# Moving q transposes, casts, a weight load and two batches' loads in a hand-ordered attention + FFN kernel

## The chip, the cores and the metric

The kernel runs on one core of one Trainium2 chip. The time is the device time of one launch in microseconds (us), the median of several runs. The engines are TensorE (PE: matmuls and transposes; its weight loads are listed apart as PEld), VectorE (DVE), ScalarE (ACT), GpSimd (POOL) and SyncE (SP). POOL and SP also issue DMAs, each into a queue of its own: the loads of this kernel go by POOL, the DMA transposes and the stores by SP. An engine works through its own instructions in order; a wait of one holds all that stand behind it on that engine.

## The reference, cut to what matters

```python
batch, n_heads, seq, head_dim = 8, 8, 576, 64
scores = q @ k.transpose(0, 1, 3, 2) / sqrt(D)
rel = pos[:, None] - pos[None, :]
mask_plain = (rel >= 0) & (rel < 32)                        # heads 0 to 3
mask_dil = (rel >= 0) & (rel < 128) & (rel % 4 == 0)        # heads 4 to 7
attn = softmax(where(mask, scores, -1e9))
x = (attn @ v).transpose(0, 2, 1, 3).reshape(4608, 512)     # 8 batches of 576 tokens
out = relu(x @ w_in) ** 2 @ w_out                           # w_in 512 x 2048, w_out 2048 x 512
```

Inputs are float32 in HBM; the matmuls run in bf16, and the loads cast on the way. The output is float32, 4608 x 512.

## The kernel before, in words

**Two halves laid into each other.** The FFN takes nearly all of PE's time; the attention of the eight batches supplies its input, xT (four slices kt of 128 rows, one for each pair of heads: 0 and 1 are the plain heads, 2 and 3 the dilated ones). The first 1024 tokens are four FFN tiles of 256 tokens, the rest tiles of 512. `ffn_groups` (L909) gives the groups of one tile: those of its first half, `g1` (L961), call `mm1` (L924), which multiplies w_in by xT over the four kt (the matmul is L937), then takes relu on ACT (L950) and the square on DVE (L953) into h2T; those of its second half, `g2`, multiply h2T by w_out (L983), copy PSUM to osb (L989) and store it on SP (L906). A tile of 256 tokens has 8 + 8 groups, one of 512 has 16 + 16. For the first two tiles the order is given by hand (`groups[:NF]` and the line behind it), and g1's first groups there take two u (two PSUM tiles pf) at once, and only two of the four kt: in the first tile groups 0 and 1 are the plain and the dilated kt of the first two u, and so on. So g1 can start when part of xT is there. The relus and squares of the first two u are not made at once but held, and let go by the code r (both relus, on ACT) and R (both squares, on DVE).

**Who sets the order.** At the end of the kernel a loop goes over the groups. After each it runs the codes of one cell of the string PROGRAM, and the steps of a list (`natural_step`, L674) that are due. PROGRAM's cells are split by "|"; the first runs before group 0, the next after group 0, and so on:

```python
    program = [x.split() for x in PROGRAM.split("|")]
    for code in program[0]:
        run(code)
    for g, group in enumerate(groups):
        ...
        group()
        for code in program[g + 1] if g + 1 < len(program) else ():
            run(code)
        while steps and steps[0][0] <= g:
            natural_step(*steps.pop(0)[2:])
```

What a code issues goes to the engines' instruction streams in that order; the codes that bear on the change are these.

- **Batch 0, part by part** (`first_step`): a code has a letter, a pair of heads 0 to 3, and a part of the tokens (0 is the first 256, 1 the rest). T transposes q and k on PE (L761, 16 transposes for q and 16 for k; "q" or "k" behind the code takes one alone); C copies the transposed halves from PSUM (DVE; an "a" behind it puts it on ACT, a "v" on DVE); S scores, E their Exp on ACT (L821) and the mask, P probabilities times v, D sums, L the Ln on ACT (L874), X the Exp of its negative (L877), M the product that writes xT on DVE (L884).
- **Casts**: h and j copy v's parts, loaded aside, into the block-diagonal vbd on DVE; j is two copies (L1096). G spreads a dilated v (L229).
- **Warm-up and filling** (`turn`, L731): s28x183 is 28 matmuls of 183 columns on an idle tile; w and W are single ones of 512 and 256 columns.
- **Loads**, codes that begin with L and a batch. q loads q and k of some pairs (L171, one DMA for q and one for k, 128 to 320 KB); v loads v, with "d" for the dilated heads and "p" for the plain ones (L192: four DMAs, two of each plain pair); V loads v of a later batch by `load_v_rows` ("d" is L465 and L470; "0" and "1" are the plain pairs 0 and 1, L478, eight DMAs for a pair). i and o load a quarter of w_in (L1055; "a" and "b" are the halves with kt 0, 1 and kt 2, 3) and of w_out (L1061). All of these are issued by POOL. x is the four DMA transposes of a batch's q and k, by SP (`cross`, L238), once its loads have landed. f loads the mask mask_n, by SP.

**The later batches.** Transposed q and k (qx, kx) are arranged by copies for the matmuls: L492 and L494 for the bulk, and the codes R for the ends of the rows, whose four pairs of DVE copies (L500 for q, L503 for k) write the tile that the trace calls kbd. `quadrants` issues the 64 x 64 matmuls of scores, sums and products (L661, into pa, pd and po); E is Exp (L698) and a mask product on DVE (L700, from batch 4 on by mask_n for the plain heads), and Ln, Exp, xT are L684 and the lines up to L689. Batch 3's copies R run near 83 us of the profiled execution, when POOL begins to issue batch 4's q and k loads; batch 4's R copies run before 111 us.

In this order POOL issues, around 70 to 90 us: L3:Vd0 (batch 3's dilated v and plain pair 0), L4:q00123 and L4:q10123 (batch 4's q and k, four DMAs), L3:V1 (batch 3's plain pair 1, eight DMAs). Ten groups later SP issues L4:x, and two cells on f.

Of the kernel before, what the change touches and what calls it, by code (L numbers as in the profile page):

```python
# [18 lines left out]


PROGRAM = (
    "L0:q001 L0:q023 L0:q123 L0:v0d L0:i0 L0:q101 L0:v1d L0:i1a L0:i1b L0:v1p L0:i2a L0:i2b L0:i3 L0:o0 L0:o1 L0:o2 L0:o3 "
    "L1:q00123 z y L1:v0dp L1:q10123 s28x183 T00 C00a T10 C10a B00 B10 w1 S00 E00 B20 W1 S10 E10 N u B30 W1 w1 T20q "
    "w1 T20k C20v T30 C30v h W1 w1 S20 E20 w1 S30 E30 T21 C21v T31 C31a G20 G30 P00 P10 D00 D10 L00 X00 P20 P30 "
    "D20 D30 L20 X20 M00 j S21 S31 w1+31 M20 E21 E31 G21 G31a | | T01 C01v r T11 C11a R P21 P31 D21 D31 S01 S11 L21 "
    "X21 M21 L31 X31 M31 E01 E11 | L2:q00123 L2:q10123 L1:v1dpr | | P01 D01 L01 X01 M01 P11 D11 L11 X11 M11 | | | "
    "| | | | | | | | | m n | | | | | | 1q1 1q3 | 1q2f 1k2f | 1k1a 1v3 | 1a2 | 1v2 1k0a 1q0v | 1o2 | 1a0 1a1 | 1k3 "
    "1o0 1o1f | 1a3 1Q0 | 1K0 1o3 | 1Q1 1K1 | 1Q2 | 1b0 | | 1Q3 1K2 L2:vwp L3:q00123 L3:q10123 L2:vwdr | L2:x | | "
    "| | 1V2 | 1b2 1p0 | 1b1 1V3 1K3 | L3:x | 1p2 1p1f | 1b3 | 2t0 2t1 1p3f | | | L3:Vd0 L4:q00123 L4:q10123 "
    "L3:V1 | | | | | | | | | | L4:x | | f | | | | | | | | | | | | | | | | L4:Vd L5:q10123 L5:q00123 L4:V01 | | | "  # L30
    "| | | | | | | | | | | | | L5:x | L5:Vd L6:q10123 L6:q00123 L5:V01"
)

# [29 lines left out]
def kernel(  # L63
# [21 lines left out]
    NE = H // 2  # L85
# [89 lines left out]
    def crossed(b: int, e: int):  # L175

        return int(b == XB and e in (1, 3) or b >= NATURAL and e == 1 or b >= PAIRED and e == 0)

    def load_v(b: int, parts, which="pdr"):


        dst = vbd[b % 2]
        if b not in vds:
            vds[b] = vd_pool.tile([P, NE // 2, 2, RES * D], bf16, name="vd")
        p0, p1 = parts[0], parts[-1] + 1
        i0, i1 = 4 * p0, 4 if p1 == 1 else NB
        sides = [(hl, slice(64 * hl, 64 * hl + 64)) for hl in range(2)]
        for what in which:
            if what == "p":
                for e in range(NE // 2):  # L190
                    for hl, rows in sides:
                        nc.gpsimd.dma_start(  # L192
                            dst[rows, e, i0:i1, rows],
                            v[b, 2 * e + (hl ^ crossed(b, e)), 64 * i0 : 64 * i1, :].rearrange("(i p) d -> p i d", p=64),
                        )
            elif what == "d" and len(parts) == 1:
                for hl, rows in sides:
                    nc.gpsimd.dma_start(
                        vds[b][rows, :, p0, :],
                        v[b, H // 2 + hl : H : 2, 256 * p0 : 256 * p1, :].rearrange("e (p r) d -> p e (r d)", r=RES),  # L200
                    )
            elif what in "d01":
                for e in (0, 1) if what == "d" else (int(what),):
                    for hl, rows in sides[::-1] if crossed(b, e + NE // 2) else sides:
                        hl = hl ^ crossed(b, e + NE // 2)
                        nc.gpsimd.dma_start(
                            vds[b][rows, e, :, :],
                            v[b, H // 2 + 2 * e + hl, 0:512, :].rearrange("(m p r) d -> p m (r d)", p=64, r=RES),
                        )
            elif b == XB:  # L210
                for g, rows in sides:
                    for i in (0, 8):
                        nc.gpsimd.dma_start(
                            dst[rows, NE // 2 : NE, i, rows],
                            v[b, H // 2 + g : H - g : 3 - 2 * g, 64 * i : 64 * i + 64, :].rearrange("h p d -> p h d"),
                        )
            elif p1 == 2:
                for hl, rows in sides:
                    nc.gpsimd.dma_start(
                        dst[rows, NE // 2 : NE, 8, rows],  # L220
                        v[b, H // 2 + hl : H : 2, 512:S, :].rearrange("h p d -> p h d"),
                    )
# [686 lines left out]
    def ffn_groups(tk0: int, nt: int):  # L909
# [6 lines left out]
        kts = (2, 0, 3, 1) if tk0 > 3 * NT else (2, 3, 1, 0) if tk0 == 2 * NT else (2, 3, 0, 1) if tk0 == 3 * NT else (0, 2, 1, 3) if NT <= tk0 < 2 * NT else (0, 1, 2, 3) if tk0 == 0 else (2, 3, 0, 1)  # L916
# [7 lines left out]
        def mm1(u, ks):  # L924
            if u not in acc:
                acc[u] = ps_f.tile([P, NT], f32, name="pf")
            for x in range(per):
                f = per * u + x
                piece = max(y for y in range(len(w_in_sb)) if w_cuts[y] <= P * f)
                c0 = 512 * (f // 4) + f % 4 - w_cuts[piece]  # L930
                for kt in ks:
                    t0 = tk0 % RING
                    to, rhs = acc[u][:, nt * x : nt * x + nt], xT[:, kt, t0 : min(t0 + nt, RING)]
                    if over:
                        to = to.rearrange("p (a t) -> p a t", a=2)
                        rhs = xT[:, kt, :].rearrange("p (a t) -> p a t", t=half)[:, 0 : t0 // half + 1 : t0 // half, :]
                    nc.tensor.matmul(  # L937
                        to,
                        w_in_sb[piece][:, kt, c0 : c0 + 509 : 4],
                        rhs,  # L940
                        start=(kt == kts[0] and x == 0),
                        stop=(kt == kts[-1] and x == per - 1),
                        skip_group_check=True,
                    )
            if ks[-1] != kts[-1]:
                return
            hv = h2[:, per * u : per * u + per, 0:nt]

            def relu():
                nc.scalar.activation(hv, acc[u][:, :].rearrange("p (x n) -> p x n", x=per), ACT.Relu)  # L950

            def square():
                nc.vector.tensor_tensor(out=hv, in0=hv, in1=hv, op=ALU.mult)  # L953

            if tk0 == 0 and u < 2:
                held.append((relu, square))
            else:
                relu()
                square()

        def g1(i):  # L961
            if i < 2 and tk0 < NT or i < 6 and tk0 == 0:
                x, y = divmod(i, 2)
                for u in (2 * x, 2 * x + 1):
                    mm1(u, kts[2 * y : 2 * y + 2])
            elif i < 2 and early:
                for u in (2 * i, 2 * i + 1):
                    mm1(u, kts[:cut])
            elif i < 4 and early:
                for u in (2 * i - 4, 2 * i - 3):  # L970
                    mm1(u, kts[cut:])
            else:
                mm1(i, kts)

        def g2(m, part):
# [11 lines left out]
            if f1 == NF:  # L987
# [3 lines left out]
                for x in (c0, DM // 2) if c1 - c0 == DM and tk0 == NTOK - NT else (c0,):  # L991
                    store(osb, pos, x, DM // 2 if x < c0 + DM // 2 and c1 - c0 == DM and tk0 == NTOK - NT else c1)

        return [lambda i=i: g1(i) for i in range(NF // per)] + [
            lambda m=m, part=part: g2(m, part) for m in range(nt // P) for part in range(4)
        ]
# [146 lines left out]
    for b in range(NATURAL, B):  # L1143
        t = G * (b - 1)
# [11 lines left out]
        if b < PAIRED:  # L1156
            start = 61 if early else t - 8
            second = t + (7 if early else 5)
            x = 3 if early else 0
# [89 lines left out]
```

## Time and profile before

| | us |
|---|---|
| runs | 298.61, 300.05, 300.09; median 300.05 |
| profiled execution, own time | 299.26 |
| profiled execution, span of the trace | 297.5 |
| PE busy in matmuls | 289.4 (97% of the span), 3150 instructions |
| of it L937 (w_in) and L983 (w_out) | 128.1 and 127.5 |
| ACT, DVE, POOL busy | 192.2 (65%), 168.5 (57%), 129.8 (44%) |
| L478, v loads, 80 issues on POOL | 43.4 |
| L171, q and k loads, 18 issues of q and 18 of k | 13.0 and 12.7 |
| granted clock of PE, mean | 0.997 of full speed |

The span runs from the first to the last recorded work; the execution's own time holds 1.76 us around it. All times of single instructions below are of this one profiled execution and count from the start of its span. "Busy" of an engine does not mean that it bounds: PE's waits, and what ended them, tell where work of others sets the time. The lines of a page's part 5 read: line of the kernel, engine, operation, what it writes <- what it reads, count, then busy time and mean of one in ns, then idle time of the engine just before, with what ended most of it. The rows of a wait list read: engine, tile and line that waited <- what it waited for (engine, tile, line), then the total in us, how often, and the longest. The rows of a timeline read: start in us, length in us, engine, line, operation, output <- input, shapes.

### The profile page before, as it was taken

Reading aid. Unit: us, or ns where it says so; the run is one execution under the profiler, and the core shown is the slowest. Engines: PE = TensorE matmul, PEld = TensorE weight load, DVE = VectorE, ACT = ScalarE, POOL = GpSimd, SP = SyncE. Lnnn points to the kernel's source line nnn. Section 1 sums busy time; section 2 is a strip of 40 time slices with the busy share of each in tenths; the row PEclk is TensorE's granted clock in tenths of the full one; section 3 lists DMA queues with packets and bytes.
Section 4 is the critical chain, followed back from the end, with each engine's and each line's share of the span. In section 5 each row is a group of like instructions: output and inputs, shape, how many; then the busy total and the mean of one; then the engine's idle time right before and its main releaser. Section 6 shows DMA issues by size and latency. Waiting matters only on the chain.

```text
span 297.5 us, 7863 instructions
## 1 busy us (share of the span) xinstructions
PE 289.4 (97%) x3150; PEld 169.2 (57%) x3177; DVE 168.5 (57%) x508; ACT 192.2 (65%) x397; POOL 129.8 (44%) x210
## 2 busy tenths in 40 slices
PE   8999999999999999999999999999999999999994
PEld 7689657869655554555455445545554555445443
DVE  2785566977879665686749474957445234004400
ACT  6898568767948665888667667766676567126511
POOL 8679883666786467564782697100000000000000
PEclk9999999999999999999999999999999999999998
DMA  8999999999999999969999499112101200121022
GB/s 126 196 168 213 205 156 228 187 175 167 186 132 171 178 166 168 196 95 147 156 192 151 61 177 167 10 37 73 37 0 35 75 35 0 37 71 35 0 74 71
DMA packets 83156, 35.37 MB, mean 119 GB/s; under 512 B 52656, under 2 KB 78512, under 8 KB 83120
## 3 DMA queue, kind: packets, MB, share of 16 engines
q0 software_dynamic: 49024, 18.40, 53.9%
q1 hardware_dynamic: 33952, 16.38, 26.3%
q8 instruction: 25, 0.41, 0.5%
q10 hardware_dynamic: 144, 0.10, 0.1%
q14 instruction: 11, 0.09, 0.1%
HBM read 37.31 MB, written 9.44 MB: 157 GB/s over the span
## 4 chain that ended last, share of the span: by engine, by line
PE 90%; DVE 3%; ACT 2%; DMA 2%; issue 1%; POOL 1%; ACTq 0%; POOLq 0%; DVEq 0%
PE pf L937 41%; PE pf L983 40%; DMA kb<-in_k_dram 2%; PE po L661 2%; PE pa L661 1%; PE pf L661 1%; PE pa L277 1%; PE pa L761 1%; DVE xT L884 1%; PE pd L661 1%; DVE kbd L503 0%; ACT rec L684 0%; POOL qb L171 0%; DVE h2T L953 0%; ACT h2T L950 0%
## 5 line engine op out<-in xcount | busy, mean ns | idle before, releaser
L937 PE MATMUL pf<-xT,w_in 128*128 128x512 bf16 (+1 forms) x697 | 128.1, 340 | 0.7 <-DVE xT L884 0.2
L983 PE MATMUL pf<-w_out_sb,h2T 128*128 128x512 bf16 (+2 forms) x572 | 127.5, 373 | 1.3 <-issue 0.5
L937 PEld LDWEIGHTS <-w_in 128*128 128x128 bf16 x704 | 77.9, 113 | 47.0 <-issue 1.1
L950 ACT ACTIVATE h2T<-pf 128x512 bf16<-128x512 f32 x144 | 83.7, 600 | 29.5 <-PE pf L937 29.3
L953 DVE TENSOR_TENSOR h2T<-h2T 128x512 bf16<-128x512 bf16 x144 | 60.3, 425 | 60.1 <-ACT h2T L950 57.7
L983 PEld LDWEIGHTS <-h2T 128*128 128x128 bf16 x592 | 55.6, 98 | 61.5
L478 POOL DMA_DIRECT2D vbd<-in_v_dram x80 | 43.4, 556 | 23.4 <-DMA kb<-in_k_dram 9.0
L989 ACT COPY osb<-pf 128x512 f32<-128x512 f32 (+1 forms) x34 | 19.5, 573 | 49.7 <-PE pf L983 46.6
L171 POOL DMA_DIRECT2D qb<-in_q_dram x18 | 13.0, 721 | 11.4 <-DMA xx<-qb 9.4
L684 ACT ACTIVATE rec<-rec 128x576 f32<-128x576 f32 x24 | 16.4, 682 | 0.7
L698 ACT ACTIVATE pt<-pa 128x384 bf16<-128x384 f32 (+1 forms) x28 | 12.7, 498 | 6.2 <-DVE xT L689 3.7
L192 POOL DMA_DIRECT2D vbd<-in_v_dram x16 | 10.9, 690 | 7.6 <-DMA kb<-in_k_dram 2.9
L465 POOL DMA_DIRECT2D vd<-in_v_dram x20 | 12.2, 621 | 4.0 <-DMA vbd<-in_v_dram 2.7
L687 DVE TENSOR_TENSOR xT<-po,rec 128x512 bf16<-128x512 f32 x14 | 9.7, 691 | 7.5 <-ACT rec L684 7.1
L171 POOL DMA_DIRECT2D kb<-in_k_dram x18 | 12.7, 705 | 1.9 <-issue 0.7
L700 DVE TENSOR_TENSOR pt<-pt,mask_n 128x448 bf16<-128x448 bf16 (+1 forms) x20 | 7.1, 373 | 9.5 <-ACT pt L698 9.4
L470 POOL DMA_DIRECT2D vbd<-in_v_dram x20 | 12.2, 628 | 0.1
L700 DVE TENSOR_TENSOR pt<-pt,mask_f 128x384 bf16<-128x384 bf16 x24 | 8.4, 355 | 6.0 <-ACT pt L698 5.8
L687 DVE TENSOR_TENSOR xT<-pf,rec 128x512 bf16<-128x512 f32 x10 | 6.9, 692 | 8.4 <-ACT rec L684 8.4
L492 DVE COPY qT<-xx 64x576 bf16<-64x576 bf16 (+1 forms) x30 | 10.7, 357 | 0.6
L661 PEld LDWEIGHTS <-vbd 64*64 64x64 bf16 x288 | 7.6, 107 | 4.2 <-issue 3.8
L698 ACT ACTIVATE pt<-pf 128x448 bf16<-128x448 f32 (+1 forms) x18 | 8.5, 521 | 0.5 <-PE pf L661 0.3
(156 smaller groups left out, 317.7 us busy)
## 6 DMA issues: line engine op xcount, KB each, us to landing
qb<-in_q_dram POOLq DMA_DIRECT2D x7, 320.0 KB, 7.2
kb<-in_k_dram POOLq DMA_DIRECT2D x7, 320.0 KB, 7.9
vd<-in_v_dram POOLq DMA_DIRECT2D x32, 64.0 KB, 4.8
w_out_sb<-in_moe_w_out_dram POOLq DMA_DIRECT2D x4, 512.0 KB, 11.5
out_dram<-osb SPq DMA_DIRECT2D x16, 128.0 KB, 4.9
qb<-in_q_dram POOLq DMA_DIRECT2D x7, 256.0 KB, 6.8
kb<-in_k_dram POOLq DMA_DIRECT2D x7, 256.0 KB, 8.5
out_dram<-osb SPq DMA_DIRECT2D x9, 160.0 KB, 3.1
```

The lines of the kernel that those rows point to most:

```text
L171: nc.gpsimd.dma_start(t[0:n, part, hs, :], src[b, hs, t0 : t0 + RES * n, :].rearrange("h (p r) d -> p h (r d)", r=RES))
L478: nc.gpsimd.dma_start(v_rows[b % 2][p0 + 16 * r : p0 + 16 * r + 16, e, :, :], v[b, 2 * e + hl, :, :].rearrange("(i m r) d -> r m i d", r=R ...
L661: nc.tensor.matmul(out, lhs, rhs, start=begin, stop=True, skip_group_check=True)
L684: nc.scalar.activation(rec[:, :], rec[:, :], ACT.Exp, scale=-1.0)
L687: nc.vector.tensor_tensor(out=tok[:, :, 16:M], in0=byr(o[:, :]), in1=byr(rec[:, 0:512]), op=ALU.mult)
L698: nc.scalar.activation(pt, sp[b, e][g][:, 0:n], ACT.Exp, scale=SCALE)
L700: nc.vector.tensor_tensor(out=pt, in0=pt, in1=mask, op=ALU.mult)
L937: nc.tensor.matmul(to, w_in_sb[piece][:, kt, c0 : c0 + 509 : 4], rhs, start=(kt == kts[0] and x == 0), stop=(kt == kts[-1] and x == per - ...
L950: nc.scalar.activation(hv, acc[u][:, :].rearrange("p (x n) -> p x n", x=per), ACT.Relu)
L953: nc.vector.tensor_tensor(out=hv, in0=hv, in1=hv, op=ALU.mult)
L983: nc.tensor.matmul(cur[m][:, c0:c1], h2[:, f, P * m : P * m + P], w_out_sb[:, f, c0:c1], start=(f == 0), stop=(f == NF - 1),)
L989: (nc.vector.tensor_copy if last and part == 1 or tk0 == 3 * NT // 2 else nc.scalar.copy)(osb[:, c0:c1], cur[m][:, c0:c1])
```

## The change

1. The warm-up is 34 matmuls of 151 columns instead of 28 of 183.
2. The load of batch 0's later plain v (L0:v1p, four DMAs) is split into its pairs, "s" and "t" (two DMAs each), which `load_v` now takes. The first half of w_in's third quarter (L0:i2a) is issued between them: v pair 0, i2a, v pair 1, i2b instead of v pairs 0 and 1, i2a, i2b.
3. The two casts j go from behind M00 (xT of pair 0, part 0) to between C21v and T31, that is on DVE ahead of the copy C31 and of all products of part 0.
4. The q transposes of the plain pairs' second part, T01q and T11q, go from behind group 1 to between group 0 and group 1; the k transposes T01k and T11k stay behind group 1. The two held relus r go from between C01v and T11 to behind C11a, and so behind it on ACT.
5. In the second tile (tokens 256 to 511, kt order 2, 3, 0, 1) the group g1(1), which adds kt 0 and kt 1 to the first two u, goes kt by kt: the four matmuls of kt 0 for both u, then the four of kt 1, instead of u by u with kt 0 and kt 1 in turn. In the trace of before its first two matmuls start at 24.53 and 24.88.
6. L3:V1, eight DMA issues, goes ahead of L4:q00123 and L4:q10123 on POOL.

Nothing is added to or taken from what is computed.

```diff
-    "L0:q001 L0:q023 L0:q123 L0:v0d L0:i0 L0:q101 L0:v1d L0:i1a L0:i1b L0:v1p L0:i2a L0:i2b L0:i3 L0:o0 L0:o1 L0:o2 L0:o3 "
-    "L1:q00123 z y L1:v0dp L1:q10123 s28x183 T00 C00a T10 C10a B00 B10 w1 S00 E00 B20 W1 S10 E10 N u B30 W1 w1 T20q "
-    "w1 T20k C20v T30 C30v h W1 w1 S20 E20 w1 S30 E30 T21 C21v T31 C31a G20 G30 P00 P10 D00 D10 L00 X00 P20 P30 "
-    "D20 D30 L20 X20 M00 j S21 S31 w1+31 M20 E21 E31 G21 G31a | | T01 C01v r T11 C11a R P21 P31 D21 D31 S01 S11 L21 "
+    "L0:q001 L0:q023 L0:q123 L0:v0d L0:i0 L0:q101 L0:v1d L0:i1a L0:i1b L0:v1s L0:i2a L0:v1t L0:i2b L0:i3 L0:o0 L0:o1 L0:o2 L0:o3 "
+    "L1:q00123 z y L1:v0dp L1:q10123 s34x151 T00 C00a T10 C10a B00 B10 w1 S00 E00 B20 W1 S10 E10 N u B30 W1 w1 T20q "
+    "w1 T20k C20v T30 C30v h W1 w1 S20 E20 w1 S30 E30 T21 C21v j T31 C31a G20 G30 P00 P10 D00 D10 L00 X00 P20 P30 "
+    "D20 D30 L20 X20 M00 S21 S31 w1+31 M20 E21 E31 G21 G31a | T01q T11q | T01k C01v T11k C11a r R P21 P31 D21 D31 S01 S11 L21 "
...
-    "| | 1V2 | 1b2 1p0 | 1b1 1V3 1K3 | L3:x | 1p2 1p1f | 1b3 | 2t0 2t1 1p3f | | | L3:Vd0 L4:q00123 L4:q10123 "
-    "L3:V1 | | | | | | | | | | L4:x | | f | | | | | | | | | | | | | | | | L4:Vd L5:q10123 L5:q00123 L4:V01 | | | "
+    "| | 1V2 | 1b2 1p0 | 1b1 1V3 1K3 | L3:x | 1p2 1p1f | 1b3 | 2t0 2t1 1p3f | | | L3:Vd0 L3:V1 L4:q00123 L4:q10123 "
+    "| | | | | | | | | | L4:x | | f | | | | | | | | | | | | | | | | L4:Vd L5:q10123 L5:q00123 L4:V01 | | | "
...
-            if what == "p":
-                for e in range(NE // 2):
+            if what in "pst":
+                for e in {"p": (0, 1), "s": (0,), "t": (1,)}[what]:
...
         def g1(i):
             if i < 2 and tk0 < NT or i < 6 and tk0 == 0:
                 x, y = divmod(i, 2)
-                for u in (2 * x, 2 * x + 1):
-                    mm1(u, kts[2 * y : 2 * y + 2])
+                for ks in [kts[2:3], kts[3:]] if tk0 and y else [kts[2 * y : 2 * y + 2]]:
+                    for u in (2 * x, 2 * x + 1):
+                        mm1(u, ks)
```

## The prediction

> **What bounds the kernel now.** First the page's part 1 and part 4, for who is busy and who stands on the chain of work that ended last; then PE's waits; then timelines of the two stretches where PE waits.
>
> ```profile
> PE 289.4 (97%) x3150; PEld 169.2 (57%) x3177; DVE 168.5 (57%) x508; ACT 192.2 (65%) x397; POOL 129.8 (44%) x210
> ...
> PE 90%; DVE 3%; ACT 2%; DMA 2%; issue 1%; POOL 1%; ACTq 0%; POOLq 0%; DVEq 0%
> ```
>
> PE is the bound: no edit takes PE work away, so only its 8 us of waits can be won. They are, from PE's waits:
>
> ```profile
> PE po L731 <- DVE kbd L1005: 1.1, 1, 1.1
> PE pa L661 <- DVE kbd L503: 0.5, 1, 0.5
> PE pf L983 <- issue: 0.5, 3, 0.2
> PE pf L813 <- issue: 0.4, 1, 0.4
> PE pf L937 <- DVE xT L884: 0.2, 1, 0.2
> PE pa L761 <- DMA kb<-in_k_dram: 0.2, 1, 0.2
> ```
>
> The first is the start, before any edit. Two of the others lie where edits bear: L937 on xT (15.90 us) and, the largest, L661 on the kbd copies of L503 (84.75 us). From DVE's timeline, columns start, length, what (pairs of L500 and L503 copy the ends of batch 3's q and k), and POOL's:
>
> ```profile
> 77.90 0.19 DVE L500 COPY kbd<-xx 64x128 bf16<-64x128 bf16 x1
> 78.01 0.30 DVE L503 COPY kbd<-xx 64x128 bf16<-64x128 bf16 x1
> ...
> 83.39 0.58 DVE L503 COPY kbd<-xx 64x128 bf16<-64x128 bf16 x1
> 83.98 0.19 DVE L500 COPY kbd<-xx 64x128 bf16<-64x128 bf16 x1
> 84.09 0.60 DVE L503 COPY kbd<-xx 64x128 bf16<-64x128 bf16 x1
> ```
> ```profile
> 82.46 0.70 POOL L171 DMA_DIRECT2D qb<-in_q_dram  x1
> 83.14 0.69 POOL L171 DMA_DIRECT2D kb<-in_k_dram  x1
> 83.81 0.76 POOL L171 DMA_DIRECT2D qb<-in_q_dram  x1
> 84.54 0.75 POOL L171 DMA_DIRECT2D kb<-in_k_dram  x1
> 85.25 2.70 POOL L478 DMA_DIRECT2D vbd<-in_v_dram  x5
> ```
>
> The same copy takes 0.30 us in general (L503: 294/303/604 ns least, median, most) and 0.58 and 0.60 only here, beside POOL's issues of L171, batch 4's q and k loads. PE waits for the second of these to end. That is the stall that the moved loads touch.
>
> **The change part by part.**
>
> *Warm-up, 34 matmuls of 151 columns for 28 of 183.* The 28 take 4.47 us, 153 ns apart, 0.84 ns a column. 34 x 151 = 5134 columns against 5124: 0.01 us. Twelve more PE instructions stand ahead of everything, so the 0.44 "issue" wait at 13.97, which no semaphore explains, may move. It is worth nothing either way: the first FFN group starts at 14.63 behind xT (L884, 13.89 + 0.69 = 14.58), whose DVE and ACT chain does not need that matmul. Value 0; ends 0 and, if it came to lie where nothing covers it, 0.44 lost.
>
> *The two casts (j, L1096) ahead of batch 0's last k cast, and the q transposes between groups 0 and 1.* Now xT of heads 0 to 3 ends at 14.58, j takes 0.29 and 0.22, and the xT of the dilated heads runs 15.15 to 15.84; PE has stood 0.24. Moved to 12.05, the casts fall into 0.39 us of idle DVE ahead of L770 and 0.15 us more; L229's first copy, 0.45 against 0.22 for the next, ends with POOL's L192 as it does now, so xT moves by 0 to 0.1. The second xT is then ready by 15.6, and PE, with 16 transposes (0.31) in between, comes at about 16.1: no wait, 0.24 won. The price is one more turn between L937 and the 64-row L761: the rows leave 0.09 ahead of the transposes and 0.10 behind them, 0.19 in all. Sum 0.05 won.
>
> *Relus (r) behind C11a on ACT.* Now the two relus (1.08) run at 16.82, C11a at 17.79, and L874 at 18.54 after 0.31 idle. As built, C11a comes first and waits for the transposes of k, which end at about 17.6; C11a 0.43, two relus 1.08: L874 at about 19.1, 0.5 late. Queued behind it on ACT are Ln, Exp and the scores' Exp; xT of head pair 3 (20.34 to 20.83) ends at about 21.3, and group 4's second matmul reads it at 21.08. PE would wait 0.2 to 0.4. PSUM of the two relus comes free at 19.1, just as the next pair needs it (19.2). Value 0.3 lost; ends 0 and 0.45.
>
> *Pair by pair order in the four groups of g1(1) at token 256.* Now the second matmul there starts 0.35 behind the first (24.53, 24.88), where 0.11 is the pace: 0.24 of wait for xT of pair 1 (L884, 24.33 + 0.49 = 24.82). Four matmuls of pair 0 first give 0.44 of cover. 0.24 won, as long as the Ln/Exp chain is late only by what PE is.
>
> *Half of w_in[2] ahead of v's second pair.* The bytes ahead of the second half stay, so it lands as before (needed at 23.65); the first half lands 0.5 sooner, needed 22.8; the v pair 1.3 later, at about 22.2, needed at 22.3. PE never waited for w_in here. Value 0; ends 0 and 0.2 lost.
>
> Front: 0.05 - 0.3 + 0.24, so **about 0**, ends -0.6 and +0.3. A loss is not eaten later: from 25.6 to 84 PE hardly waits.
>
> *Batch 4's q and k loads behind batch 3's v (L3:V1).* Eight issues of L478, 0.53 each, come at 82.46 and L171 only at 86.7. Beside the copies POOL then runs L478. Bounds for a copy beside L478, by its rows: 0.30 (106.51, 109.92), 0.33 (77.08), 0.40 (110.34). Two copies at 0.30 to 0.40 for 0.58 and 0.60: 0.4 to 0.6 less. PE's wait in pace is 0.69 (84.06 to 84.75), so all of it counts. Value **0.5 won**.
>
> *What that makes late.* The loads issue 4.3 later, but land less than that later: the rings run at 30 to 52 GB/s from 82 to 85 us and two stores (SP, 83.4) are out of the way. kb's first part now takes 5.9 us (issue 83.14; POOL's wait for it ends at 89.3); the fastest 128 KB loads of the start took 4.4. It lands 2.8 to 4.3 later; I take 3. SP's transposes wait for it (89.08, four, SP's last ends at 97.92), the mask_n load (97.97, 4.3 to landing, 102.3) is queued behind them, stores behind that. With 3 more, less some competition, it lands at 104.9 (104.2 to 106.6). Who waits: DVE's L700 on pt and mask_n, now at 104.43, and behind it the copies of batch 4's ends, xT, and three more pairs, the last ending at 110.74; PE reads that at 110.92. DVE idles 1.45 in between (108.26, for ACT), so the mask may land at 105.8 for nothing, at 105.4 with PE 0.5 sooner. Value 0; ends 0 and 1.2 lost. Batch 5's loads start about 3 later, its transposes (now 115.42, behind stores) under 1; its copies at 131 have 3 us of slack. v's second pair comes sooner and is needed only at 110.
>
> [...]
>
> **Sum.** 0 + 0.5 - 0 (0.1 at a mean over the mask's ends): 0.45 won. Against the profiled execution (297.5 span, 299.26 with what lies around it): 298.8. That execution lies 0.79 under the median of the three runs (300.05) and between them (298.61 to 300.09); the middle of all four is 299.65, so I forecast **299.2** for a median.
>
> **The rivals** (times on the same footing as 299.2).
> *A. L478 holds the copies as long as L171.* For: 0.43 and 0.40 us in two rows of a copy that meets the end of an issue, and back-to-back issues always offer one. Against: most rows at 0.30. Only the front is left: 299.65.
> *B. The mask comes late; slower.* It decides from 105.9: there the stall of L661 at 110.9 equals what was won at 84.75. For: the transposes of batch 3 took 67.8 to 76.7 on SP and more to land, some 2 us longer than batch 4's, in rings as full. With loads 3.6 later and such transposes the mask lands at 108.0, L700 to the last pair takes 2.0 + 0.43 + 1.10 + 1.37, PE reads at 113.0 for 110.92: 2.1 lost, 301.7. Against: rings are emptier then.
> *C. The relus cost nothing*, because C11a gets its transposes sooner or the late xT is hidden: front +0.3, in all 0.8 won, 298.9.
> That the change does not do what it says: the built order shows each move; of the casts alone PE's 0.24 would be gone.
>
> **How the numbers follow.** Forecast 0.5, A 0.15, B 0.15, C 0.2. 8 in 10: C's 298.9 with the runs' spread (0.75 either way) below, half of B left out above: 298.1 to 300.9. Half a per cent, 1.5 us, is about what a measurement of this kernel can tell from no change. No case wins 1.5; a median's spread on C gives faster 0.1. B is 1.65 over 300.05: slower 0.1. Within: 0.8.
>
> **What would show it.** L503 at 83.4 and 84.1 at 0.30 to 0.40, L661's wait on it under 0.2; L937's wait at 15.90 gone, the pause at 24.88 gone; L874 at 19.1 and a wait of L937 at 21; L171 at 86.7, mask_n landing near 104.9, no wait of L661 near 110.5. It is wrong if L503 stays at 0.58 (A), if L661 waits at 110 to 113 (B), or if PE's total wait falls by over 1 us.

## The result, and the profile after

The changed kernel takes 301.17 us (median of 19 runs, 299.70 to 304.32), the kernel before beside it 299.40 (19 runs, 298.48 to 301.79): ratio 1.0061, 95% interval 1.0039 to 1.0084. It is 0.6% slower, where 299.2 was forecast, and the time lies outside the range (298.1 to 300.9). Slow runs, over 1.5% above the fastest of their kernel, are left out of the ratios here and below: one of these 19 (304.32), and three of the six with the mask loaded three times. The execution that was profiled is the fastest of the 19: its own time is 299.70, its span 297.9.

First the page of the changed kernel, parts 1 and 4. From L966 on a line's number is higher by one than before (L983 is now L984).

```profile
PE 290.1 (97%) x3156; PEld 169.6 (57%) x3183; DVE 167.7 (56%) x508; ACT 192.0 (64%) x397; POOL 129.3 (43%) x210
...
PE 75%; DMA 13%; POOL 5%; DVE 2%; issue 2%; ACT 1%; SPq 0%; ACTq 0%; DVEq 0%; POOLq 0%
```

No engine's busy time moved by more than 0.8 us, but the chain that ended last did: before, PE held 90% of it and DMA 2%, now PE holds 75% and DMA and POOL 18%. So the chain leaves PE somewhere. Its pieces in order of time (start, length, what) show where it comes back:

```profile
88.20 7.50 DMA qb<-in_q_dram
...
95.98 5.91 DMA vbd<-in_v_dram
101.89 0.38 SPq L238
102.33 4.01 DMA mask_n<-near_by_residue
106.43 0.67 DVE pt L700 x2
...
108.76 0.69 DVE xT L687
...
110.88 0.42 DVE kbd L503
111.34 0.22 PE pa L661 x3
111.72 5.99 PE pf L984 x27
```

PE is late at 111.34 because the last copy L503 ends at 111.30, and that stands on DVE behind L700, which waited for mask_n. The mask is issued at 102.33 and lands at 106.34; L700 begins 0.09 later, as it does in the three other traces in which the mask is late. (The timeline of this one execution names ACT's L680 for that wait, which happened to end at 106.35; the first experiment tells the two apart.) In the profile of before the mask landed at 102.29, and L700 waited for ACT's Exp (L698) until 104.43. SP's queue in the two kernels, before first, says why the mask is late (start, length, line):

```profile
89.08 1.24 SPq L238 DMA_TRANSPOSE xx<-kb  x1
90.41 3.07 SPq L238 DMA_TRANSPOSE xx<-qb  x1
93.59 2.63 SPq L238 DMA_TRANSPOSE xx<-kb  x1
96.31 1.61 SPq L238 DMA_TRANSPOSE xx<-qb  x1
97.97 1.15 SPq L1100 DMA_DIRECT2D mask_n<-near_by_residue  x1
```
```profile
92.35 1.84 SPq L238 DMA_TRANSPOSE xx<-kb  x1
94.28 3.69 SPq L238 DMA_TRANSPOSE xx<-qb  x1
98.07 2.74 SPq L238 DMA_TRANSPOSE xx<-kb  x1
100.90 1.37 SPq L238 DMA_TRANSPOSE xx<-qb  x1
102.33 1.27 SPq L1101 DMA_DIRECT2D mask_n<-near_by_residue  x1
```

What SP waited for before the first of them, in the changed kernel (from 86 to 108 us):

```profile
SPq L238 <- DMA kb<-in_k_dram: 7.9, 1, 7.9
```

The four transposes begin 3.27 later, behind kb's later landing (92.30 for 89.03), take 9.92 instead of 8.84 from the first start to the last end, and the mask is queued behind them. The chain above goes back from the last transpose to a load of vbd; SP's queue does not bear that out, since each transpose there starts within 0.1 of the end of the one before.

What was to be won at 84.75 was won. DVE's copies of the same ends in the changed kernel, now beside POOL's L478, not L171:

```profile
83.19 0.18 DVE L500 COPY kbd<-xx 64x128 bf16<-64x128 bf16 x1
83.29 0.30 DVE L503 COPY kbd<-xx 64x128 bf16<-64x128 bf16 x1
83.60 0.19 DVE L500 COPY kbd<-xx 64x128 bf16<-64x128 bf16 x1
83.71 0.30 DVE L503 COPY kbd<-xx 64x128 bf16<-64x128 bf16 x1
```

And PE's waits no longer name L503 at 85:

```profile
PE po L731 <- DVE kbd L1006: 1.1, 1, 1.1
PE pf L937 <- DVE xT L884: 0.6, 1, 0.6
PE pf L984 <- issue: 0.5, 3, 0.2
PE pa L761 <- DMA kb<-in_k_dram: 0.3, 1, 0.3
```

The 0.6 on xT is the first FFN matmul, at 14.70: the wait of 0.44 at 13.97 that the profile of before calls "issue" is gone, and PE waits for the same xT as before. The list does not name the loss at 111, because it is spread over a row of matmuls. Between the FFN matmuls on its two sides, the block of L661 takes from 110.06 to 111.29 before, 1.23, and now from 109.50 to 111.72, 2.22. Its matmuls wait one after the other for DVE, none of them for long.

The sum, from the start of the same FFN matmuls in both traces: the first FFN matmul 0.07 later, 0.18 won from there to 25 us, 0.58 won at 85, 1.11 lost at 111: 0.42 later to the end, which is the 0.4 between the spans. That is the fastest of 19 executions; the median lies 1.5 above it.

### The profile page after: what moved, and what is told of

Read it like the earlier page. It is cut to its first block, busy times and chain, and to the rows that moved or that the text cites. A ratio compares the mean times of both kernels' runs of the same rounds, so it can differ in the third digit from the quotient of the medians.

```text
span 297.9 us, 7875 instructions
## 1 busy us (share of the span) xinstructions
PE 290.1 (97%) x3156; PEld 169.6 (57%) x3183; DVE 167.7 (56%) x508; ACT 192.0 (64%) x397; POOL 129.3 (43%) x210
## 4 chain that ended last, share of the span: by engine, by line
PE 75%; DMA 13%; POOL 5%; DVE 2%; issue 2%; ACT 1%; SPq 0%; ACTq 0%; DVEq 0%; POOLq 0%
PE pf L937 34%; PE pf L984 34%; DMA kb<-in_k_dram 5%; DMA vbd<-in_v_dram 5%; DMA qb<-in_q_dram 3%; POOL vbd L478 2%; DMA mask_n<-near_by_residue 1%; PE po L661 1%; POOL qb L171 1%; PE pf L661 1%; PE pa L661 1%; PE pa L761 1%; PE pa L277 1%; ACT h2T L950 1%; POOL vbd L192 0%
## 5 line engine op out<-in xcount | busy, mean ns | idle before, releaser
L984 PE MATMUL pf<-w_out_sb,h2T 128*128 128x512 bf16 (+2 forms) x572 | 127.5, 373 | 1.3 <-issue 0.5
L984 PEld LDWEIGHTS <-h2T 128*128 128x128 bf16 x592 | 55.6, 98 | 61.5
L478 POOL DMA_DIRECT2D vbd<-in_v_dram x80 | 42.9, 546 | 20.2 <-DMA qb<-in_q_dram 8.0
L171 POOL DMA_DIRECT2D qb<-in_q_dram x18 | 12.9, 718 | 12.8 <-DMA xx<-qb 11.3
L698 ACT ACTIVATE pt<-pa 128x384 bf16<-128x384 f32 (+1 forms) x28 | 12.8, 499 | 6.1 <-DVE xT L689 3.6
L470 POOL DMA_DIRECT2D vbd<-in_v_dram x20 | 12.0, 614 | 6.0 <-DMA qb<-in_q_dram 2.6
L700 DVE TENSOR_TENSOR pt<-pt,mask_n 128x448 bf16<-128x448 bf16 (+1 forms) x20 | 7.0, 372 | 12.1 <-ACT pt L698 7.4
L171 POOL DMA_DIRECT2D kb<-in_k_dram x18 | 12.9, 716 | 1.8 <-issue 0.8
L687 DVE TENSOR_TENSOR xT<-po,rec 128x512 bf16<-128x512 f32 x14 | 9.7, 691 | 5.6 <-ACT rec L684 5.3
L465 POOL DMA_DIRECT2D vd<-in_v_dram x20 | 12.1, 617 | 1.4 <-DMA vbd<-in_v_dram 1.3
L700 DVE TENSOR_TENSOR pt<-pt,mask_f 128x384 bf16<-128x384 bf16 x24 | 8.4, 355 | 6.3 <-ACT pt L698 6.2
L687 DVE TENSOR_TENSOR xT<-pf,rec 128x512 bf16<-128x512 f32 x10 | 6.9, 691 | 8.8 <-ACT rec L684 8.8
L661 PEld LDWEIGHTS <-vbd 64*64 64x64 bf16 x288 | 7.9, 107 | 4.6 <-issue 3.5
L661 PE MATMUL po<-pt,vbd 64*64 64x96 bf16 (+2 forms) x188 | 8.8, 201 | 0.1
```

Of the source, the lines that this page charges most:

```text
L171: nc.gpsimd.dma_start(t[0:n, part, hs, :], src[b, hs, t0 : t0 + RES * n, :].rearrange("h (p r) d -> p h (r d)", r=RES))
L478: nc.gpsimd.dma_start(v_rows[b % 2][p0 + 16 * r : p0 + 16 * r + 16, e, :, :], v[b, 2 * e + hl, :, :].rearrange("(i m r) d -> r m i d", r=R ...
L661: nc.tensor.matmul(out, lhs, rhs, start=begin, stop=True, skip_group_check=True)
L687: nc.vector.tensor_tensor(out=tok[:, :, 16:M], in0=byr(o[:, :]), in1=byr(rec[:, 0:512]), op=ALU.mult)
L698: nc.scalar.activation(pt, sp[b, e][g][:, 0:n], ACT.Exp, scale=SCALE)
L700: nc.vector.tensor_tensor(out=pt, in0=pt, in1=mask, op=ALU.mult)
```

## The experiments

Theory M: the loss is the mask alone. It is late because its load is queued on SP behind transposes that wait for later loads; each us beyond 105.4 is lost at 111. Theory T: batch 4's later transposes themselves hold DVE, and the mask only stands beside them. Theory F: the front costs in most executions what the profiled one does not show.

**The mask load ahead of the transposes, in the changed kernel.**

```diff
-... | L4:x | | f | ...
+... | f L4:x | | | ...
```

> The changed kernel, with the load of mask_n issued by SP ahead of batch 4's four transposes and not behind them; nothing else. Theory M (the mask is late because it is queued on SP behind transposes that wait for later loads, and every us that it lands after about 105.4 is lost at the wait of L661 near 111): what was won at 84.75 (0.58) and in front (0.1) stays, and nothing is lost: 0.5 to 0.8 faster than before, L700 on mask_n about 104, no wait of L661 near 111, and a spread of runs as narrow as that of before. Theory T (batch 4's transposes themselves land too late for the copies R on DVE, and the mask only stands beside them): DVE then waits at 106 to 108 for L500 instead, and 0 to 1.5 slower than before. Theory F (the front costs in most runs what the profiled run does not show): about 1 slower than before whatever the mask does.

Measured: 298.78 (12 runs, 298.43 to 301.11), before beside it 299.56; ratio 0.9990 (0.9973 to 1.0008), so the 0.6% is gone; a gain over before is not shown, since the interval includes no change. Its DVE timeline:

```profile
103.73 0.74 DVE L700 TENSOR_TENSOR pt<-pt,mask_n 128x448 bf16<-128x448 bf16 x2 [1.94 <-ACT pt L698]
```

L700 waits for ACT again. The transposes are as late as in the changed kernel (SP's last ends at 102.33, it lands at 105.11) and PE has no wait at 111: T falls, M stands.

**The moved loads of batches 3 and 4 alone, in the kernel before.**

```diff
-... L3:Vd0 L4:q00123 L4:q10123 L3:V1 ...
+... L3:Vd0 L3:V1 L4:q00123 L4:q10123 ...
```

> The kernel before with one edit alone: L3:V1 ahead of batch 4's q and k loads. Theory M and theory T: as slow as the whole change, 1.3 to 2.2 slower than before, with the wide spread of runs, mask_n landing at 106 or later. Theory F: 0.5 faster than before or within 0.3 of it.

Measured: 302.77 (6 runs, 300.60 to 303.62); ratio 1.0108 (1.0076 to 1.0140). The mask lands at 108.58. So this part alone makes the loss; that it is larger than that of the whole change (301.17) was not expected. Its trace shows a second price, in a table of stretches (window; length, then PE, PEld, DVE, ACT, POOL busy, granted clock, DMA share, GB/s):

```profile
109.60:111.80 2.20, 0.03 (x1) 0.06 (x1) 2.13 (x9) 0.00 (x0) 1.45 (x3) 1.00 0.61 99
111.80:114.20 2.40, 2.20 (x90) 1.52 (x90) 1.63 (x8) 0.70 (x2) 2.40 (x5) 0.99 1.23 218
114.20:117.60 3.40, 3.40 (x10) 1.21 (x9) 2.13 (x6) 1.98 (x5) 1.00 (x3) 0.51 1.44 195
117.60:120.00 2.40, 2.40 (x13) 1.10 (x12) 1.14 (x4) 0.59 (x1) 0.75 (x2) 1.00 1.40 139
```

PE stands for 2.2 us, and 2.4 us after it resumes the granted clock is 0.51 for 3.4 us: eight matmuls start 0.43 apart instead of 0.22, another 1.7 lost. That the wait brought this on is my reading of this one trace.

**Everything but the moved loads.** The changed kernel with L3:V1 back behind batch 4's loads.

> The changed kernel with L3:V1 put back behind batch 4's q and k loads, so that all other parts are in. Theories M and T: within 0.3 of before, narrow spread (the profiles of the two kernels differ by 0.1 up to 84 us). Theory F: 1 or more slower than before.

Measured: 298.83 (12 runs, 298.17 to 299.50); ratio 0.9974 (0.9957 to 0.9991): faster, where M had "within 0.3" and F "1 slower". F falls. The mask lands at 103.11, in time. This is the one of twelve comparisons that is faster clear of its interval.

**The changed kernel once more.**

> The changed kernel once more, for the profile of another execution and beside the other three on one chip. All theories: 1.2 to 2.4 slower than before. Theory M: where its time is above that of the first profile (299.70), the mask_n load lands later than 106.34 by as much, and the wait of L661 near 111 is longer by as much. Theory F: the more lies ahead of 84 us.

Measured: 300.41 (12 runs, 298.93 to 302.22); ratio 1.0029 (1.0000 to 1.0058). That is 0.9 above before's 299.56 in this set, less than any theory had, and about half the loss of the first measurement (1.0061); between the two sets the size of the loss is not settled better than 0.3 to 0.6%. The profiled execution, 301.39, has the mask at 107.76, 1.42 later than the first profile, and PE's wait list names L661:

```profile
PE po L661 <- DVE xT L687: 1.1, 1, 1.1
```

At 111 it lost 2.1, against 1.1: 1.0 more for 1.42 of the mask, with PE 0.6 later there, so that the mask was due later too. Most of the rest of its 1.69 lies at the start (first FFN matmul at 15.25 for 14.70), which is F's place and not M's.

**The mask load first, in the kernel before.** The edit of the first experiment, in the kernel before.

> The kernel before with one edit: the load of mask_n ahead of batch 4's transposes on SP. Theory M (only the mask's lateness costs; where the kernel before runs over 301 it was late there too): the median within 0.4 below that of before, no run over 300.5. Theory S (the kernel before has its own slow executions for another reason, as in its front): the same median and as many runs over 300.5 as before has (8 of 29). Rival to M on this point: a transfer of 114 KB at 84 us in the way of batch 4's loads makes it slower by up to 0.5.

Measured: 299.25 (12 runs, 298.61 to 300.63), before 299.30; ratio 0.9997 (0.9978 to 1.0016). Two of the 12 runs lie over 300.5, where M had none; of before, two of 29 do in this set, and five of 29 in the set that the expectation counts (not eight). So it is S on this point: in the old order the mask is rarely the limit, and three of 12 runs over 300 with the mask first show that such runs have other causes too. The rival's 0.5 is not there.

**The relus back ahead of C11a**, in the changed kernel with the mask first.

```diff
-T01k C01v T11k C11a r R
+T01k C01v r T11k C11a R
```

> The changed kernel with the mask load first and the two relus r put back ahead of C11a on ACT. Term of the relus as predicted (0.3 lost; 0.21 in the traces so far, between the groups at 19.2 and 21.1): the time from the first FFN matmul to 25 us is 0.2 to 0.3 shorter than with the relus behind C11a, and the whole 0.2 to 0.3 faster than the kernel with the mask load first (298.78), so 298.5. If the late xT is hidden anyway: no difference.

Measured: 299.13 (12 runs, 298.33 to 300.56); ratio to before 0.9991 (0.9973 to 1.0010), for the whole time no difference that can be told. The trace tells it: from the first FFN matmul to the 111th (near 30.6 us) it takes 15.67, and 15.85 or 15.86 in all six traces with the relus behind C11a, and PE's wait near 21 is gone. The term is 0.18.

**The mask load twice, and three times, in the kernel before.**

```diff
-... | L4:x | | f | ...
+... | L4:x | | f f | ...
+... | L4:x | | f f f | ...
```

> The kernel before, with the load of mask_n issued twice in a row on SP (the second waits for the first to land, and L700 for the second); load order and all else as before. It delays the mask alone, with batch 4's loads and transposes where they were. Theory M: the last landing is near 105.5 to 106.5; the wait at 110.9 is 0 to 0.6 and the time 0 to 0.6 above that of before, with more runs above 301. Theory T (it is batch 4's loads and transposes that count): no difference from before.

Measured: 299.79 (12 runs, 298.62 to 303.00); ratio 1.0018 (0.9994 to 1.0043). The mask lands at 105.91, and nothing is lost at 110. That does not test the bound, because PE came there 1.15 later than in the profile of before: it had waited 1.1 before 77.95, where batch 2's dilated v came late (L213, issued at 71.18, landed at 77.91; in the profile of before the last of them landed at 74.92):

```profile
PE po L661 <- DMA vbd<-in_v_dram: 1.1, 1, 1.1
```

> As the one with two loads, with three. Theory M: the last landing near 109, so PE waits about 3 us at 110; and where PE stands over some 2 us, the granted clock falls to half for 3 to 4 us behind it, which costs 1.7 more (as in the profile of the loads moved alone): 3 to 5 us above before, mean clock 0.993 or 0.994. Without the clock's step: 2.5 to 3 us. Theory T: no difference from before.

Measured: 307.03 (6 runs, 302.33 to 309.19); ratio 1.0148 (1.0098 to 1.0199), over the runs from 302.33 to 306.24. Theory T, "no difference", falls here too. With loads and transposes in their old places, the mask alone, landing at 110.54, does this to DVE:

```profile
110.63 0.66 DVE L700 TENSOR_TENSOR pt<-pt,mask_n 128x448 bf16<-128x448 bf16 x2 [7.28 <-DMA mask_n<-near_by_residue]
```

and PE stands 2.71 before 113.71, and loses 3.6 in all there. (The profile puts this wait to a load of vbd, but the last that PE can need there landed at 102.52; DVE's product L687, behind the mask, ends at 113.66.) This execution (303.60) kept its clock at 1.00 behind that wait, so I was wrong that it must fall; the six runs' mean clocks are 0.983 to 0.998.

**What else was in the front.** The kernel without the moved loads was 0.26% faster than before, 0.8 us, of which the front explains 0.18 in the profiled pair. Four last kernels ask which edit does it, and whether the mask load first adds to it.

```diff
 kernel before, half w_in alone:   -L0:v1p L0:i2a L0:i2b   +L0:v1s L0:i2a L0:v1t L0:i2b
 front without half w_in:          changed kernel, L3:V1 back and L0:v1p L0:i2a L0:i2b back
 loads and half w_in:              kernel before, L3:V1 moved and L0:v1s L0:i2a L0:v1t L0:i2b
 front, mask first:                changed kernel, L3:V1 back, f ahead of L4:x
```

> The kernel before with one edit: batch 0's plain v loaded pair by pair with half of w_in's third quarter between the pairs. What is open: the changed kernel without the moved loads was 0.26% faster than before, its traced front only 0.18 us; and in the traces of all kernels with the new front POOL comes to batch 3's first L470 at 70.9 to 71.8, with the old front at 71.6 to 74.6. Theory H (the order of the loads on POOL does both): 0.4 to 0.8 faster than before, L470 at 70.9 to 71.8. Theory O (the edits on PE, DVE and ACT do it): as before, 299.4, L470 between 71.6 and 74.6. Theory N (chance): as before, L470 anywhere between 70.9 and 74.6.

Measured: 299.55 (11 runs, 298.85 to 301.07); ratio 1.0002 (0.9979 to 1.0025); L470 at 71.56. H falls for the time.

> The changed kernel without the moved loads of batches 3 and 4 and without the half w_in load between v's pairs: the edits on PE, DVE and ACT alone. Theory H: 0 to 0.2 faster than before (its own gain of 0.18 in the front), L470 at 71.6 to 74.6. Theory O: 0.4 to 0.8 faster, L470 at 70.9 to 71.8. Theory N: 0.2 to 0.5 faster, L470 anywhere.

Measured: 299.23 (12 runs, 298.82 to 299.76); ratio 0.9990 (0.9973 to 1.0007); L470 at 70.71. The ratio is N's, the difference of the medians (299.33 and 299.23) H's, the L470 nearest to O's, and the interval includes no change: this decides nothing.

> The kernel before with the moved loads of batches 3 and 4 and the half w_in load; no edit on PE, DVE or ACT. With the moved loads alone: 302.77; the whole change: 301.17 and 300.41. Theory H: as slow as the whole change, 300.4 to 301.4, since POOL's stream is earlier and with it the mask. Theories O and N: as slow as the loads alone, 302 to 303.

Measured: 300.73 (12 runs, 299.37 to 303.64); ratio 1.0049 (1.0024 to 1.0074); the mask lands at 107.25 and 2.2 is lost at 111. The time is as H had it, and not as O and N had it; but POOL begins L470 at 72.55, as with the moved loads alone (72.49), so H's reason is not what the trace shows.

> The changed kernel with the loads of batches 3 and 4 as before and the mask load ahead of batch 4's transposes: the version that the runs so far point to. Theory M: the mask is early enough in it anyway, so it is as fast as the changed kernel without the moved loads (298.83), 298.4 to 298.9. A rival: the moved loads were worth their 0.3 at L661 at 85 once the mask is out of the way; then this one is 0.2 to 0.3 slower than the changed kernel with the mask first (298.78).

Measured: 298.99 (12 runs, 298.44 to 300.00); ratio 0.9987 (0.9970 to 1.0004). By the medians this is the rival (0.21 above 298.78), by the ratios to before, which were measured beside each, it is not (0.9987 and 0.9990); a difference of 0.3 is within the intervals. The one version that is faster clear of its interval stays the changed kernel without the moved loads, and of its two nearest kin (without the half w_in, with the mask first) neither is.

Over the traces, the time from the first FFN matmul to the 111th shows what the front does behind the first xT:

| | us |
|---|---|
| old front (seven traces, before among them at 16.03) | 15.91 to 16.60, mean 16.20 |
| new front (six traces) | 15.85 to 15.86 |
| new front, relus ahead of C11a (one) | 15.67 |

So counted, the new front wins 0.35 in the mean, of which the profile of before shows 0.18. The rest is a wait that this profile does not have and three of the seven with the old front do, near 19 (0.25 to 0.59). From PE's waits of the kernel with the half w_in alone:

```profile
PE pa L813 <- DVE xx L776: 0.2, 1, 0.2
```

But this count begins behind the moved casts, and so leaves out their price. From DVE's last copy L768 ahead of them to the first xT it takes 2.46 in the profile of before (11.43 to 13.89) and 2.66 in that of the changed kernel (11.30 to 13.96); the means are 2.44 and 2.55. With it, the profiled pair shows nothing won in front, and the mean some 0.2. The start itself moves by more than that from execution to execution: the first FFN matmul is at 14.13 to 14.95 with the old front and at 14.48 to 15.25 with the new.

## Why the prediction was wrong, by its own steps

**The step that failed** is "What that makes late": the mask "lands at 104.9", "Value 0". The mechanism around it held: who waits, where, and from when. The bound was 105.8 with PE where it was before, and five late landings bear it out, each us beyond it costing one. The last column takes the loss off the landing and adds how far PE was ahead of the profile of before; if the mechanism holds, it is the bound in every row (all in us):

| kernel | mask lands | PE ahead of before, at 109 us | lost at 111 | landing - lost + ahead |
|---|---|---|---|---|
| changed kernel | 106.34 | 0.69 | 1.11 | 105.92 |
| loads and half w_in | 107.25 | 0.74 | 2.17 | 105.82 |
| changed kernel, once more | 107.76 | 0.07 | 2.14 | 105.69 |
| moved loads alone | 108.58 | 0.51 | 3.22, and 1.65 of half clock | 105.87 |
| mask three times | 110.54 | -0.86 | 3.63 | 106.05 |

A mask that lands at 101.6 to 103.1, as in the old order, costs nothing (0.1 or less). What was mis-sized is the landing. In the profiled pair the mask lands at 106.34 and not at 104.9, 1.44 later: 0.27 because the transposes start 3.27 later and not 3, 1.08 because they take longer, where the forecast took them as before or a little shorter, and 0.1 for the mask's own load. Over the traces a third term comes in, the profile that the sum stands on:

| from the traces | old order (eight) | new order (six) | predicted |
|---|---|---|---|
| first transpose starts | 88.62 to 92.61, mean 90.2 | 92.26 to 96.12, mean 93.3 | 3 later: 3.1 |
| transposes, first start to last end | 8.1 to 10.1, mean 9.0 | 9.3 to 10.5, mean 9.9 | unchanged: 0.9 longer |
| last transpose leaves SP | 97.92 to 100.73, mean 99.2 | 102.17 to 105.37, mean 103.2 | 101 |

So the delay of the loads was right. That the transposes would take as long as before was not; the profile of before held a warning, since batch 3's four transposes take 10.2 there (66.46 to 76.68; the prediction's 67.8 is the start of the second). Why batch 4's take longer now stays open: they run beside POOL's L465 and L470 from their start, where a part ran beside L478 before, but whether that is the cause was not tried. And the start was not typical: 97.92 in the profile of before is the earliest of eight, 1.25 ahead of their mean. The mask itself lands at 106.34 to 108.58 in the four traces that load it there, mean 107.5, not at 104.9.

**The rivals.** This is B, which had 0.15: the mechanism, its place and its price (301.7 against 301.17 and 300.41) were there. What spoke against it, "rings are emptier then", did not help: while the four transposes run, the mean DMA share is 1.40 after and 1.51 before, and they take longer all the same. With the 3 us by which SP's last transpose moves over the eight traces, against 0.5 of slack, an even chance would have been nearer.

**L503 beside L478** held: 0.30 to 0.40 in all twelve copies of the six traces with the new order; with L171 beside them one of two copies or both take 0.47 to 0.60 in seven of the eight others. 0.58 was won for 0.5 in the profiled pair, but here too the profile of before was the far end: of the eight traces with the old order it loses most at 85, and in the mean the new order wins 0.3 there (six traces against eight). Rival A falls, and so does C, since the relus did cost. Beside L478, whose issues of 0.53 follow one another without a break, no L503 copy in any trace takes more than 0.16 over its 0.30; beside L171 it is 0.30 at most.

**The front, "about 0".** The pair order won 0.24, as worked out: the pause at 24.88 is gone. The relus cost 0.18 for 0.3; L874 begins at 18.87 for 19.1, and PE then waits 0.2 for xT at 21.25. The ACT timeline of the changed kernel:

```profile
17.59 0.42 ACT L775 COPY xx<-pa 128x320 bf16<-128x320 bf16 x1 [0.80 <-PE pa L761]
17.91 1.09 ACT L950 ACTIVATE h2T<-pf 128x512 bf16<-128x512 f32 x2
18.87 0.46 ACT L874 ACTIVATE rec<-pd 128x320 f32<-128x320 f32 x1
```

From the first FFN matmul on, the casts and q transposes won 0.15 in the profiled pair (0.10 lost to 16.1, 0.25 won to 19.2) for 0.05, and some 0.3 on average (0.35, less the pair order, plus the relus), for a wait that the one profile of before did not show. Ahead of it they cost 0.20 in that pair, where the prediction had xT move by 0 to 0.1, and 0.1 on average. "About 0" was right for the profiled pair, in part by errors that cancel. The warm-up and the half w_in were put at 0; the kernel with the half w_in alone is unchanged, the warm-up was not tried by itself.

**Left open.** Why the moved loads alone (302.77, six runs) are slower than with the half w_in beside them (300.73). Four of the six have a mean clock of 0.993 or 0.994 and take 302.69 to 303.62; the two at 0.999 and 1.000 take 300.60 and 301.24, no more than the other kernel. So most of it is how often the clock fell, one in 12 there. And POOL comes to batch 4's first L171 at 88.94 in the one and 87.41 in the other, from waits between 78 and 84 us that one trace of each does not explain. It is open too whether runs of the kernel before over 300 us are the late v at 77.95 that one trace shows.

## What to carry to other kernels

A load that is queued behind waiting DMAs has the due time of the slowest of them (in the changed kernel the mask was issued at 102.33, 0.06 behind the last of four transposes that had waited for kb until 92.30): when loads are moved, follow every queue to its last entry, and take a small constant that nothing holds out of that queue (here one word in the order undoes a loss of 0.3 to 0.6%). Take a due time with its spread over executions, not from one profile: 3 us of slack in that one was 0.5 after the shift as estimated, in a place that moves by 3. The same goes for a gain: the wait of PE at 85 was the longest of eight in the one profile. And a wait of PE can cost more than its length: in the trace of the moved loads alone the granted clock fell to 0.51 behind a wait of 2.2 us.

## What the runs showed that was not expected

The clock's fall depends on more than the length of the wait: it fell behind 2.19 us in one trace and not behind 2.71 in another. A mean clock of 0.995 or less stands in 10 of the 49 runs with the new load order and the mask behind the transposes, and in none of the 83 runs of the seven kernels with the old load order or the mask first, those with the mask loaded twice or three times aside. The kernel before shows it too, in a few runs (6 of 93 in three sets). That a wait stands ahead of each such fall is argued: one of them was traced.

A DMA issue on POOL lengthens DVE's 64x128 copy L503, and by how much depends on the issue. Over all traces the copy takes 0.32 at most where no POOL issue runs beside it (133 copies); beside L478 alone (16-row pieces of 128 bytes) 0.29 to 0.46, ten of 132 over 0.40; beside L171 alone 0.29 to 0.60, 21 of 38 over 0.40. Both kinds of issue run back to back for 0.5 to 0.9 us each. What in the issue does it was not tried.
